# Norm chunks queued behind their roots, tables and tap rows ahead of the second block, down weight pieces ahead of their row pair: one core of a Trainium2 chip

The kernel computes a layer norm, a long convolution branch, a gated MLP branch and all their gradients in one launch. The change moves work in time and adds almost none.

## The chip, the cores and the metric

The program runs on one core of a Trainium2 chip. Times are device microseconds (us) of that core. "Span" is the time of a profiled execution from its first to its last instruction. The engines are called PE (TensorE, matmuls), PEld (its weight loads), DVE (VectorE), ACT (ScalarE), POOL (GpSimd) and SP (SyncE, which issues most DMAs; SPq is its queue of issues).

## The reference

```python
def _B_ref(x, W_gate, W_up, W_down):
    gate = einsum(x, W_gate); up = einsum(x, W_up)
    return einsum(gate * (gate > 0) * up, W_down)      # relu gate
# x = A_q [1, 2048, 1024]; F = 3584; everything is bf16 ... (cut)
xn = _layernorm(x)
out = x + _A_ref(xn, A_k, A_v, A_shift_k, A_ssm_k, A_ssm_D) + _B_ref(xn, W_gate, W_up, W_down)
# _A_ref: k through a 4-tap shift per channel (shift_k), times v, a convolution of
# length 2048 with ssm_k by FFT, plus ssm_D times the same, times xn   ... (cut)
_out, _vjp = jax.vjp(f, A_q, A_k, A_v, A_shift_k, A_ssm_k, A_ssm_D, W_gate, W_up, W_down)
return (_out, *_vjp(grad_out))                          # 10 outputs
```

## The kernel before

`hidden` runs 14 blocks (2 halves of the rows by 7 column blocks of 512). In a block each of 8 row tiles of 128 gets three gemms of 8 matmuls: gate (`ps_g`), up (`ps_u`) and the gradient of the hidden layer (`ps_h`). Their results leave PSUM through four buffers: ACT evicts gate and `ps_h`, DVE evicts up (`ru`). Pieces of the A branch (`steps`) are put between the gemms from some 45 us of matmul work on. Names in the views: `xnT` and `goT` are the normalised rows and the incoming gradient, transposed; `wg`, `wu` and `wdT` the gate, up and down weights; `ru` and `gh` evicted results, which go on to the stores `ug_d` and `h_d`; `hT` is the transposed filter (`ssm_k`), `flp` a transposed intermediate of the FFT, `skb` the tap rows. The first block must also normalise its rows: 10 chunks of one or two row tiles, each loaded by SP, summed by ACT, averaged and scaled by DVE, and transposed by PE (`pst_x`).

```python
LN_CHUNKS = (1, 1, 1, 1, 2, 2, 2, 2, 2, 2)

def layer_norm(...):                       # a generator: three yields a chunk  (cut)
    for i, n in enumerate(self.LN_CHUNKS):
        for j in range(n):
            total = row_sums(j, 0, ACT.Copy)            # ACT  ln_j
        average(0, b(0))                                # DVE  ln_b <- ln_s
        ...                                             # subtract, ACT squares
        yield
        ...
        self.ln_act = nc.scalar.activation(out=f(4), in_=f(3), func=ACT.Sqrt)   # the root
        yield
        ...                                             # reciprocals, scaling on DVE
        yield

def hidden(...):                           # cut to what the change touches
    def up(s, mid=None):
        ...
        self.gemm8(ps, xT[s], wu, mid)
        V.scalar_tensor_tensor(out=ru[s][:, 1, :], in1=ps[:], ...)    # DVE evicts ps_u
    def chunk():
        for _ in range(3):
            next(ln)
    if ahead:                              # the first block
        ...
        yield from first_gate_up(0)
        yield from first_gate_up(2)
        chunk()
    for sp in range(0, HS, 2):             # pairs of row tiles
        if not ahead:
            yield from gate_up(sp)
            load_down(sp // 2)             # a piece of the next block's down weight
        yield from grad(sp)
        if ahead:
            with self.tc.issue_after(self.stored.ins):
                load(6 + sp // 2)          # norm chunks 6 to 9
                if sp == 0:
                    for q in range(4):
                        load_down(q)
        if ahead and sp + 4 < HS:
            yield from gate_up(sp + 4)
            chunk()
        if n == 1 and sp < 4:
            chunk()
            if sp == 2:
                with self.tc.issue_after(self.ln_act.ins), self.tc.issue_after(self.ln_dve.ins):
                    tables()               # DFT tables: ACT sines, DVE index arithmetic

def steps(self):                           # the A branch
    self.pin = True
    nx = self.loads_1(0)
    self.loads_2(nx)
    yield 12000
    self.shift_rows()                      # transpose the taps, copy, store to sk_d
    yield 11000
    self.load_xn(nx)
    self.load_taps(nx)                     # skb <- sk_d
    ...

# main
load(0); load(1); wg; load(2); load(3); wu; load(4); wdT       # in this order, shortened
goT = [b.load_T(g, i, "goT", 8 + i) for i in range(4)]          # transposes by DMA
load(5)
```

`issue_after(x)` lets what is built inside it stand only behind `x` in its queue. After `hidden` come `grad_down`, `grad_in`, `out_phase` and `grad_x`, which the change does not touch.

## Time and profile before

| what | before |
|---|---|
| median of the first 3 runs | 1937.75 us (1937.09 to 1940.97) |
| profiled execution | run 1939.18 us, span 1937.4 us, granted clock 0.996 |
| PE busy | 1893.5 us, with 15294 matmuls and 15526 weight loads recorded |
| DVE, ACT busy | 910.9 and 629.9 us |

PE is the bound, so the useful question is in which stage it is not busy. The view of windows of the kernel before answers that. Its columns are the window and its length, then busy us (and instructions) of PE, PEld, DVE, ACT and POOL, the granted clock of PE, the mean share of busy DMA engines, and GB/s.

```profile
20.00:40.00 20.00, 14.40 (x76) 6.89 (x77) 11.77 (x40) 11.17 (x23) 1.83 (x3) 0.91 1.13 239
40.00:60.00 20.00, 19.89 (x104) 9.57 (x105) 13.03 (x40) 12.82 (x25) 2.14 (x4) 1.00 0.96 271
...
120.00:140.00 20.00, 14.54 (x237) 6.77 (x238) 19.10 (x21) 7.63 (x11) 0.00 (x0) 0.83 0.82 159
```

Two stretches lose over 5 us each (20 to 40 and 120 to 140), and both ran at a lowered clock as well.

### The profile page before, as it was taken

The numbers are of one execution on the slowest core, as the hardware profiler recorded it, in microseconds if no ns is written. First come the engines' busy times: TensorE is split into PE (matmuls) and PEld (weight loads), VectorE is DVE, ScalarE is ACT, GpSimd is POOL, SyncE is SP. The second block draws the span as 40 slices with busy tenths as digits, with TensorE's granted clock in tenths as the row PEclk, the third lists the DMA queues.
The fourth block names the chain that finished last, engine by engine and source line by source line (L and its number), as shares of the span: only waits on it lengthen the run. The fifth ranks groups of instructions, "written<-read, shape, count | busy, mean of one in ns | idle before, by whom it ended". The sixth has DMA issues, their size and how long they took to land.

```text
span 1937.4 us, 35957 instructions
## 1 busy us (share of the span) xinstructions
PE 1893.5 (98%) x15294; PEld 883.2 (46%) x15526; DVE 910.9 (47%) x1378; ACT 629.9 (33%) x863; POOL 15.6 (1%) x38
## 2 busy tenths in 40 slices
PE   8989999999999999999999999999999999999998
PEld 3434444444444444444444444444444444444443
DVE  6677777777677764444444444410122222222222
ACT  5565355355355454344344344311000000000000
POOL 1000000000000000000000000000000000000000
PEclk9999999999999999999999999999999999999999
DMA  9974787974775882654753633384999854554451
GB/s 255 258 168 131 179 186 173 215 196 131 181 188 132 220 249 95 165 141 140 192 153 99 148 119 121 99 241 172 239 259 242 210 130 119 120 122 120 122 118 36
DMA packets 616017, 319.08 MB, mean 165 GB/s; under 512 B 450984, under 2 KB 585136, under 8 KB 615856
## 3 DMA queue, kind: packets, MB, share of 16 engines
q1 hardware_dynamic: 605360, 295.79, 62.2%
q10 hardware_dynamic: 9216, 16.78, 2.8%
q0 software_dynamic: 1280, 4.20, 0.6%
q8 instruction: 121, 1.98, 0.4%
q14 instruction: 40, 0.33, 0.1%
HBM read 141.56 MB, written 95.44 MB: 122 GB/s over the span
## 4 chain that ended last, share of the span: by engine, by line
PE 91%; issue 3%; DMA 2%; SPq 1%; DVE 1%; ACT 1%; ACTq 0%; DVEq 0%; POOLq 0%
PE ps_w L1047 19%; PE ps_x L1229 19%; PE ps_o L1195 10%; PE ps_h L805 9%; PE ps_g L805 9%; PE ps_u L805 9%; PE ps_d L1047 8%; PE ps L72 7%; PE ps_d L1060 1%; SPq L822 1%; PE ps_w L1060 1%; DMA ln_x<-in_A_q_dram 1%; DMA wg<-in_B_W_gate_dram 1%; SPq L816 0%; PE pst L308 0%
## 5 line engine op out<-in xcount | busy, mean ns | idle before, releaser
L1047 PE MATMUL ps_w<-ugs,xn_nat 128*128 128x512 bf16 x1672 | 376.6, 379 | 5.3 <-issue 3.5
L805 PEld LDWEIGHTS <-xnT 128*128 128x128 bf16 x1792 | 171.0, 98 | 211.4 <-issue 12.9
L1047 PEld LDWEIGHTS <-xn_nat 128*128 128x128 bf16 x1728 | 165.0, 98 | 199.3 <-issue 5.5
L805 PE MATMUL ps_g<-wg,xnT 128*128 128x512 bf16 x869 | 204.6, 381 | 5.0 <-issue 1.8
L805 PE MATMUL ps_h<-wdT,goT 128*128 128x512 bf16 x863 | 204.2, 381 | 4.3 <-issue 1.6
L805 PE MATMUL ps_u<-wu,xnT 128*128 128x512 bf16 x866 | 204.5, 380 | 2.4 <-issue 1.3
L1248 ACT ACTIVATE w<-xn,m 128x512 f32<-128x512 bf16 x32 | 24.3, 806 | 559.0 <-issue 317.2
L1229 PE MATMUL ps_x<-wuT,guT 128*128 128x512 bf16 x879 | 197.5, 379 | 0.9
L1229 PE MATMUL ps_x<-wgT,ggT 128*128 128x512 bf16 x878 | 197.3, 379 | 0.9
L1195 PE MATMUL ps_o<-wd,hT 128*128 128x512 bf16 x878 | 192.6, 379 | 0.9
L1047 PE MATMUL ps_d<-g_nat,hs 128*128 128x512 bf16 x741 | 167.7, 379 | 3.1 <-issue 2.5
L1195 PEld LDWEIGHTS <-hT 128*128 128x128 bf16 x896 | 87.7, 98 | 105.7
L1229 PEld LDWEIGHTS <-ggT 128*128 128x128 bf16 x896 | 87.7, 98 | 105.7
L1229 PEld LDWEIGHTS <-guT 128*128 128x128 bf16 x896 | 87.7, 98 | 105.7
L805 PEld LDWEIGHTS <-goT 128*128 128x128 bf16 x896 | 85.7, 98 | 105.1 <-issue 6.3
L319 DVE STREAM_TRANSPOSE flp<-C 128x1024 f32<-128x1024 f32 x48 | 90.5, 1932 | 83.3 <-ACT C L76 83.3
L905 DVE SCALAR_TENSOR_TENSOR ru<-ru,ps_u 128x512 bf16<-128x512 bf16 x112 | 76.7, 684 | 111.1 <-issue 41.7
L966 ACT CAST gh<-ps_h 128x512 bf16<-128x512 f32 x112 | 65.5, 585 | 172.5 <-PE ps_h L805 165.7
L1231 DVE CUSTOM_DVE_ANT_0 gx<-ps_x,gy 128x512 f32<-128x512 f32 x32 | 22.1, 692 | 201.9 <-PE ps_x L1229 192.0
L1145 ACT CAST wi<-ps_w 128x512 bf16<-128x512 f32 x108 | 63.7, 590 | 157.4 <-PE ps_w L1047 149.5
L76 ACT CAST C<-ps 128x1024 bf16<-128x1024 f32 x96 | 92.5, 1015 | 67.2 <-PE ps L72 66.1
L319 DVE STREAM_TRANSPOSE flp<-B 128x1024 f32<-128x1024 f32 x48 | 90.8, 1937 | 47.8 <-ACT B L76 47.8
(170 smaller groups left out, 1518.7 us busy)
## 6 DMA issues: line engine op xcount, KB each, us to landing
ug_d<-ru SPq DMA_DIRECT2D x112, 256.0 KB, 3.0
ugs<-ug_d SPq DMA_DIRECT2D x112, 256.0 KB, 5.6
wg<-in_B_W_gate_dram SPq DMA_DIRECT2D x56, 256.0 KB, 4.3
wu<-in_B_W_up_dram SPq DMA_DIRECT2D x56, 256.0 KB, 4.9
h_d<-ht SPq DMA_DIRECT2D x112, 128.0 KB, 1.8
hs<-h_d SPq DMA_DIRECT2D x56, 256.0 KB, 4.6
out_dram<-wi SPq DMA_DIRECT2D x56, 256.0 KB, 3.0
gt<-in_grad_out_dram SPq DMA_DIRECT2D x32, 256.0 KB, 4.8
```

The source lines that it names most:

```text
L72: self.pri.pin(self.nc.tensor.matmul(out, lhsT=lhsT, rhs=rhs, start=start, stop=stop))
L76: self.pri.pin(self.nc.scalar.copy(out=out, in_=in_))
L319: self.pri.pin(self.nc.vector.transpose(out=df[:, c0:c0 + 32, :], in_=sf[:, c0:c0 + 32, :]))
L805: self.pri.pin(self.nc.tensor.matmul(ps[:], lhsT=xT[:, kt * P:(kt + 1) * P], rhs=w(kt), start=(kt == 0), stop=(kt == self.DT - 1)), always ...
L905: self.pri.pin(nc.vector.scalar_tensor_tensor(out=ru[s][:, 1, :], in0=ru[s][:, 0, :], scalar=0.0, in1=ps[:], op0=ALU.is_gt, op1=ALU.mult))
L966: self.pri.pin(nc.scalar.copy(out=gh[:], in_=ps[:]))
L1047: self.pri.pin(self.nc.tensor.matmul(ps[:], lhsT=lhsT(st), rhs=rhs(st), start=(st == 0), stop=(st == self.ST - 1)))
L1060: self.pri.pin(self.nc.tensor.matmul(ps[i][:], lhsT=lhsT(i, st), rhs=rhs(i, st), start=(st == 0), stop=(st == self.ST - 1)))
L1145: self.pri.pin(nc.scalar.copy(out=wo[0][:, d, :], in_=ps[:]))
L1195: nc.tensor.matmul(ps[:], lhsT=hT[:, kt, :], rhs=self.wd[:, kt, oc], start=(kt == 0), stop=(kt == self.FT - 1))
L1229: nc.tensor.matmul(ps[:], lhsT=T[:, kt, :], rhs=W[:, kt, oc], start=(i == 0), stop=(i == n - 1))
L1248: nc.scalar.activation(out=w[:, oc], in_=xn[:, oc], func=ACT.Identity, scale=m[:, 5:6], bias=m[:, 4:5])
```

## The change

The intent is to close PE's waits in the first 370 us. It has four parts: (1) each norm chunk is queued behind the root of the last one, and the load of chunk 5 goes ahead of two of the gradient's transposes; (2) the tables are built in the first block; (3) the tap rows are transposed and stored at the start of the A branch; (4) pieces of the down weight are loaded ahead of their row pair.

```diff
@@ shift_rows (3)
-        self.act(sk_t[:], ps[:])
-        self.store(self.sk_d, sk_t[:])
+        self.nc.scalar.copy(out=sk_t[:], in_=ps[:])
+        return sk_t
@@ steps (3)
+        sk_t = self.shift_rows()
         self.pin = True
         nx = self.loads_1(0)
         self.loads_2(nx)
-        yield 12000
-        self.shift_rows()
-        yield 11000
+        yield 10000
+        self.load(self.sk_d, sk_t[:])
+        yield 13000
@@ hidden (1)
             def chunk():
-                for _ in range(3):
-                    next(ln)
+                with self.tc.issue_after(self.ln_act.ins):
+                    for _ in range(3):
+                        next(ln)
@@ hidden, the calls of the first block cut
@@ hidden (4)
                 if not ahead:
+                    load_down(sp // 2)
                     yield from gate_up(sp)
-                    load_down(sp // 2)
@@ hidden (2)
                 if n == 1 and sp < 4:
                     chunk()
-                    if sp == 2:
-                        with ...: tables()
+                if ahead and sp == 4:
+                    with ...: tables()
@@ main (1)
-    goT = [b.load_T(g, i, "goT", 8 + i) for i in range(4)]
+    goT = [b.load_T(g, i, "goT", 8 + i) for i in range(2)]
     load(5)
+    goT += [b.load_T(g, i, "goT", 8 + i) for i in range(2, 4)]
```

More of the change, by code (lines that the diff above doesn't have):

```diff
@@ L984, in chunk @@
             def chunk():
+                with self.tc.issue_after(self.ln_act.ins):
+                    for _ in range(3):
+                        next(ln)
+            if ahead:
+                self.warm(24)
                 for _ in range(3):
                     next(ln)
-            if ahead:
-                self.warm(24)
-                chunk()
                 next(ln)
@@ L1017, in hidden @@
                     chunk()
-                    if sp == 2:
-                        with self.tc.issue_after(self.ln_act.ins), self.tc.issue_after(self.ln_dve.ins):
-                            tables()
+                if ahead and sp == 4:
+                    with self.tc.issue_after(self.ln_act.ins), self.tc.issue_after(self.ln_dve.ins):
+                        tables()
             if last:
```

## The prediction

> **What bounds the kernel now.** I read the page first: busy time by engine, then the 40 slices.
>
> ```profile
> PE 1893.5 (98%) x15294; PEld 883.2 (46%) x15526; DVE 910.9 (47%) x1378; ACT 629.9 (33%) x863; POOL 15.6 (1%) x38
> ...
> PE   8989999999999999999999999999999999999998
> ...
> PEclk9999999999999999999999999999999999999999
> ```
>
> TensorE (PE) is busy 98% of 1937.4 us. A change that removes no matmul can win only the idle time of PE, 1937.4 - 1893.5 = 43.9 us, plus matmuls that ran at a lower clock. The slices put the idle time into the first and third slice (48 us each) and the last. The diff removes no matmul, and the two orders of PE's instructions (31054 rows in both kernels) are the same but for the place of one small transpose (of the taps) and buffer names. So the question is which waits of PE it touches. Hence the third view, who PE waited for:
>
> ```profile
> PE pst_x L834 <- DVE ln_x L786: 5.5, 3, 4.5
> ...
> PE ps L72 <- DVE flp L319: 3.2, 1, 3.2
> ...
> PE ps_g L805 <- DVE ru L905: 1.6, 1, 1.6
> ...
> PE ps_h L805 <- DMA wdT<-in_B_W_down_dram: 1.4, 1, 1.4
> ...
> PE ps L72 <- ACT hT L76: 1.2, 1, 1.2
> ```
>
> The columns are total us, times, longest. The rest of PE's list is gaps of 0.2 us ("issue"), and some 8 us lie in the tail after the last matmul; the change touches neither. These five waits are the whole field, and each is aimed at by one part of the diff. Fourth view, the timeline around the two largest; PE first, at 27 us:
>
> ```profile
> 27.50 1.89 PE L805 MATMUL ps_h<-wdT,goT 128*128 128x512 bf16 x8
> 33.92 1.30 PE L834 MATMUL pst_x<-ident,ln_x 128*128 128x128 bf16 x16 [4.54 <-DVE ln_x L786]
> 35.02 2.34 PE L805 MATMUL ps_h<-wdT,goT 128*128 128x512 bf16 x5
> ```
>
> and all engines in the same stretch, for the cause:
>
> ```profile
> 30.91 1.06 ACT L742 ACTIVATE ln_j<-ln_x 128x1024 bf16<-128x1024 bf16 x1 [3.44 <-DMA ln_x<-in_A_q_dram]
> ...
> 31.96 0.19 ACT L774 ACTIVATE ln_s<-ln_s 128x2 f32<-128x2 f32 x1
> ```
>
> The 0.19 us square root (L774) of norm chunk 4 stands on ScalarE behind the first row sum of chunk 5, whose data was issued at 25.50 and landed at 30.9. The root's input was ready at 27.58 (the cast before it on VectorE ends there). The 16 transposes of PE wait for that chunk. Next, the stretch before 135 us, first the cause on VectorE, then PE:
>
> ```profile
> 115.94 1.23 DVE L80 TENSOR_TENSOR ksh<-kp,skb 128x2048 bf16<-128x2048 bf16 x1 [6.92 <-DMA skb<-sk_d]
> ```
>
> ```profile
> 122.50 1.89 PE L805 MATMUL ps_g<-wg,xnT 128*128 128x512 bf16 x8 [1.59 <-DVE ru L905]
> 127.61 1.06 PE L72 MATMUL ps<-flp,FW 64*32 64x128 bf16 x64 [3.23 <-DVE flp L319]
> 129.00 3.19 PE L805 MATMUL ps_g<-wg,xnT 128*128 128x512 bf16 x7 [0.33 <-issue]
> ```
>
> VectorE stood 6.92 us for the tap rows (skb): stored at 109.51, loaded at 113.03. From there it is solidly busy (9.93 of 10 us in 120 to 130), and PE waits for it twice.
>
> **What the Trainium skill says.** (1) "TensorE: Matmul & The Clock Gate", Part 1 (the HAM clock gate): after about one 3.4 us window of idleness the array runs at half clock, 426.7 ns from matmul to matmul at 512 columns instead of 215.7. The trace agrees: 8 in 1.73 us normally (216 ns), but 5 in 2.13 us (426 ns) by the chain of waits after the 4.54 us gap. So a long wait costs more than its length. After the pair 1.59 + 3.23 us it slowed as well, though each is under 3.4; after the lone 1.42 us wait at 366 us it did not. (2) "Perfetto Trace Analysis", Per-engine timelines: VectorE and ScalarE execute strictly in order. The root that is stuck behind a row sum is that. (3) "ScalarE: Activation LUTs", What ACT_TABLE_LOAD costs: about 1283 ns per switch of set, plus a drain. The trace has 1.28 us for the load at 95.44, with the sine 0.02 us after it, so no drain is seen.
>
> **The change part by part.** A full-clock gemm of 8 matmuls is 1.73 us; I measure each loss against that.
>
> *Norm chunk behind the root, sixth load ahead of two gradient transposes.* From ps_h at 27.50 to the first gate matmul at 38.23 is 10.73 us; the work is 2 x 1.73 + 0.89 (16 transposes) = 4.35. Loss 6.38: 4.54 of waiting and some 1.8 of half clock. After: root at about 27.7; then on VectorE in the new order reciprocal (0.16), a small one (0.15), ru (0.69), a small one, ht (0.42), two small ones, with gaps about 2.2 us in all, so the scaling starts near 30.0 and PE's transposes (0.5 after it) near 30.5. PE is ready at 29.2. A wait of about 1.2 us stays, too short for the gate. **Saved: 5.2.**
>
> *Tables earlier.* Before, they ran at 93 to 109 us between the last norm chunk and the first filter work. At 102.02 the copy of hT on ScalarE, whose transposes were done at 101.0, came behind a sine of 1.15 us. In the new order no sine stands there. **Saved: about 1.0 of the 1.2.** VectorE loses 16 us of crowding (9.63 and 8.62 of 10 us busy in 90 to 110). The price: norm roots now fall between sines; ScalarE has 5 table loads instead of 2, 3 x 1.28 = 3.8 us. They fall near 60 to 92 us, where ScalarE is busy 3 to 6 of 10 us, and PE has four PSUM buffers of 1.73 us each before a late eviction stops it. I follow the new order there: evictions come 0.6 to 1.5 us late, with over 3 us to spare. **Cost on the path: 0.**
>
> *Tap rows early.* From ps_h at 119.01 to the second group of flp matmuls at 134.60 is 15.59 us. The work is 2 x 1.73 plus 4.24 (the same group and two gemms in the next round, 134.60 to 138.84) = 7.70. Loss 7.9: 1.8 and 3.4 of waiting, 2.7 of half clock. After: skb lands near 102, so gt, ksh and the taps follow PE's evictions; I put the second flp of VectorE about 2 us ahead of PE's need. **Saved: 7.9.**
>
> *Down weight pieces ahead of their pair.* The wait of 1.42 at 366 us: the piece was issued at 362.49, after two 1.3 us transposes of xn, and needed at 364.6. Ahead of the pair it is there about 7 us earlier. **Saved: 1.4.** The other 55 pieces were hidden already.
>
> Sum: 5.2 + 1.0 + 7.9 + 1.4 = 15.5, so 1937.75 - 15.5 = 1922.3. I add 1.2 for small new waits: **1923.5 us**.
>
> **The rivals.** *A DMA takes the place.* In the first 75 us the DMA engines are busy about all the time (mean share 1.0 to 1.2), and PE comes 5 us earlier. Gate weights of block 1 land about 60 and are needed at 63.3; those of block 2 are issued from 100.34 and needed from 108.67, and the last norm chunk, which the token load ahead of them on the queue waits for, may be 1 us later. Against it: most of these transfers wait for PE to free their buffers and so move with it, and the load queue had some 3 us of idle time at 48 to 53. Worth +1 to +5: about 1927. *VectorE stays the bound at 120 us*: if the taps start only 4 us earlier, PE still waits 2 us and may fall to half clock: +3 to +5, 1927. *The gap at 30 us stays long*, if chunk 4's root waits for something else: +5, 1928. *All is gained*: 6.4 + 1.2 + 7.9 + 1.4 = 16.9 gives 1920.9, the floor. *Table switching stalls PE*: needs an eviction over 3 us late; then 1.28 us per switch, +2 to +4.
>
> **Range and chances.** Two per cent is 38.8 us, over twice all that can be won, and the after-story changes nothing past the first 400 us but DMA order. So within 2% is nearly certain: faster 0.01, same 0.985, slower 0.005. The low end is the floor less 2 us of run spread (before: 1937.1 to 1941.0); the high end has two rivals come true: 1918.5 to 1931.
>
> **What the profile after would show.** PE's wait for ln_x falls from 4.5 to about 1.2; waits for flp, skb and wdT are gone; the clock near 35 and 130 us is full; the tables stand near 60 to 85 us; busy PE stays about 1890 while the span falls 14 us. I am wrong if PE has a new wait over 1 us for wg, wu or goT in the first 130 us, if a wait for ru or gh near 65 to 95 appears, or if the busy time of VectorE still touches PE at 120.

## The result, and the profile after

The changed kernel took 1930.61 us (median of 4 runs, 1927.86 to 1934.58), the kernel before 1937.66 us (4 runs, 1937.09 to 1940.97). The ratio is 0.9962, with a 95% interval of 0.9941 to 0.9982. The result is within 2% and inside the predicted range, but 7 us above the predicted point: about half of the predicted 14.2 us came.

The profiled execution has a span of 1928.7 us at a clock of 0.998. The page of the changed kernel begins with the busy times:

```profile
PE 1909.5 (99%) x15526; PEld 881.6 (46%) x15526; DVE 910.5 (47%) x1378; ACT 633.8 (33%) x866; POOL 15.3 (1%) x38
```

PE's busy time seems to have *grown* by 16 us, with no matmul added. The counts explain it: 15526 matmuls for 15526 weight loads here, but only 15294 for 15526 in the trace of before. That trace had lost 232 matmul records. The second trace of the changed kernel (a0_after, below) settles it: with 15294 matmuls recorded too, PE is busy 1891.9 us there, in a span of 1929.1 us. So a lost record reads as idle time of PE (some of it as the 0.2 us "issue" waits, of which the full trace has none), and the 43.9 us of idle time were overstated by some 17.6 us, what the two traces of one kernel differ by. PE's busy totals can be compared only between traces with equal counts. Stages of the first 140 us can, where few records are lost. The windows of the changed kernel:

```profile
20.00:40.00 20.00, 18.45 (x103) 8.73 (x102) 13.77 (x45) 12.03 (x24) 2.68 (x5) 1.00 1.11 236
40.00:60.00 20.00, 16.62 (x82) 7.63 (x80) 11.16 (x34) 12.38 (x24) 1.07 (x2) 0.91 1.07 288
...
120.00:140.00 20.00, 20.00 (x337) 9.49 (x335) 12.86 (x15) 13.43 (x18) 0.00 (x0) 1.00 0.88 167
```

The bad stretches of before are repaired: PE rose from 14.40 to 18.45 us and from 14.54 to 20.00 us of 20, at full clock. But 40 to 60, which was full, now has the hole and the lowered clock (0.91, just what 20 to 40 had before). The list of PE's waits in the changed kernel (total us, times, longest) names it:

```profile
PE ps_h L806 <- DVE ru L906: 3.4, 1, 3.4
PE pst_x L835 <- DVE ln_x L787: 2.4, 4, 0.8
PE ps_u L806 <- DMA wu<-in_B_W_up_dram: 1.7, 1, 1.7
...
PE ps L72 <- ACT hT L76: 0.2, 1, 0.2
```

The long wait for `ln_x`, and the waits for `flp` and `wdT`, are gone; the one for `hT` has shrunk to 0.2. In their place stand one of 3.4 us for `ru` and one of 1.7 us for `wu`. PE's timeline of the changed kernel around the first (start, length, instructions, the wait before them in brackets):

```profile
27.02 1.89 PE L806 MATMUL ps_h<-wdT,goT 128*128 128x512 bf16 x8
29.67 1.07 PE L835 MATMUL pst_x<-ident,ln_x 128*128 128x128 bf16 x16 [0.76 <-DVE ln_x L787]
...
40.98 1.06 PE L835 MATMUL pst_x<-ident,ln_x 128*128 128x128 bf16 x16
45.41 3.56 PE L806 MATMUL ps_h<-wdT,goT 128*128 128x512 bf16 x8 [3.38 <-DVE ru L906]
48.77 3.67 PE L806 MATMUL ps_g<-wg,xnT 128*128 128x512 bf16 x16
```

The norm gap is down to 0.76 us. PE therefore reaches the `pst_x` of the next tile at 40.98; before it was there at 46.86, about 6 us later. Then it waits 3.38 us, and its next gemm runs at half clock (3.56 us in place of 1.89). The same stretch on the other engines tells why:

```profile
28.18 6.91 SPq L823 DMA_TRANSPOSE goT<-in_grad_out_dram  x4
...
36.29 0.41 SPq L723 DMA_DIRECT2D ln_x<-in_A_q_dram  x1
...
41.26 1.06 ACT L743 ACTIVATE ln_j<-ln_x 128x1024 bf16<-128x1024 bf16 x1 [4.66 <-DMA ln_x<-in_A_q_dram]
...
43.48 0.17 DVE L757 TENSOR_SCALAR ln_b<-ln_s 128x2 bf16<-128x2 f32 x1 [4.54 <-ACT ln_j L743]
...
44.69 0.68 DVE L906 SCALAR_TENSOR_TENSOR ru<-ru,ps_u 128x512 bf16<-128x512 bf16 x1
```

Read it from the top. Four gradient transposes hold SP for 6.91 us, stores follow, and SP issues the load of norm chunk 6 at 36.29; it lands at about 41.2. ACT waits 4.66 us for it, and DVE waits for ACT's sums. Behind that average (L757), in DVE's order, stands `ru` (L906), the eviction that must free the PSUM buffer for PE's `ps_h`. So DVE stands idle with an eviction in its queue, and PE waits behind it. In the kernel before the same queue and the same engine show:

```profile
27.61 7.20 SPq L822 DMA_TRANSPOSE goT<-in_grad_out_dram  x4
...
36.07 0.40 SPq L722 DMA_DIRECT2D ln_x<-in_A_q_dram  x1
```

```profile
42.38 1.05 ACT L742 ACTIVATE ln_j<-ln_x 128x1024 bf16<-128x1024 bf16 x1
```

The load was issued at 36.07, behind four gradient transposes that hold SP for 7.20 us and behind stores, and in the changed kernel it comes at the same time (36.29, behind the same transposes). But before, ACT came to it at 42.38 and found it there. The compute moved about 6 us earlier and the load did not.

The stretch of the taps (PE, changed kernel) has no wait left:

```profile
118.13 1.90 PE L806 MATMUL ps_h<-wdT,goT 128*128 128x512 bf16 x8
...
121.69 0.75 PE L72 MATMUL ps<-flp,FW 64*32 64x128 bf16 x64
...
125.93 0.75 PE L72 MATMUL ps<-flp,FW 64*32 64x128 bf16 x64
```

From `ps_h` to the second `flp` group it is 125.93 - 118.13 = 7.80 us, where it was 15.59.

The balance of the two profiles, each gap against its work as the prediction counts it:

| stretch | loss before | loss after | saved | predicted |
|---|---|---|---|---|
| norm chunk at 30 us | 6.38 | 0.97 | 5.4 | 5.2 |
| `hT` at 102 us | 1.19 | 0.23 | 1.0 | 1.0 |
| taps at 120 us | 7.89 | 0.10 | 7.8 | 7.9 |
| `wdT` at 366 us | 1.42 | 0 | 1.4 | 1.4 |
| start (first loads, differs from run to run) | | | 0.5 | |
| chunk 6 at 42 us: wait 3.4, half clock 1.6, rest 0.2 | 0 | 5.2 | -5.2 | |
| weights: `wu` 1.7 at 257 us, `wg` 0.8 at 108 us | 0 | 2.5 | -2.5 | |
| sum | | | 8.4 | 15.5, less 1.2 |

The spans differ by 1937.4 - 1928.7 = 8.7 us, so the balance closes within 0.3 us. (5.2 is 7.79 us from 40.98 to 48.77 less 16 transposes, 0.89, and one gemm, 1.73. The 0.8 for `wg` is read from the time between the third and the fourth pair of `hT` matmuls, with one gate gemm between them: 106.60 to 109.52 is 2.92 us, and before it was 108.23 to 110.39, 2.16 us. The list of waits shows only 0.2 of it.)

### The profile page after: what moved, and what is told of

It is laid out like the page before. It is cut to its first block, busy times and chain, and to the rows that moved or that the text cites. A ratio compares the mean times of both kernels' runs of the same rounds, so it can differ in the third digit from the quotient of the medians.

```text
span 1928.7 us, 36213 instructions
## 1 busy us (share of the span) xinstructions
PE 1909.5 (99%) x15526; PEld 881.6 (46%) x15526; DVE 910.5 (47%) x1378; ACT 633.8 (33%) x866; POOL 15.3 (1%) x38
## 4 chain that ended last, share of the span: by engine, by line
PE 96%; issue 1%; DMA 1%; DVE 1%; ACT 1%; DVEq 0%; SPq 0%; ACTq 0%
PE ps_w L1050 20%; PE ps_x L1232 19%; PE ps_o L1198 10%; PE ps_h L806 10%; PE ps_u L806 10%; PE ps_g L806 10%; PE ps_d L1050 9%; PE ps L72 7%; PE ps_d L1063 1%; PE ps_w L1063 1%; ACT ln_j L743 0%; PE pst L308 0%; DMA ln_x<-in_A_q_dram 0%; DMA wu<-in_B_W_up_dram 0%; DMA wg<-in_B_W_gate_dram 0%
## 5 line engine op out<-in xcount | busy, mean ns | idle before, releaser
L1050 PE MATMUL ps_w<-ugs,xn_nat 128*128 128x512 bf16 x1728 | 383.7, 379 | 0.0
L1050 PE MATMUL ps_d<-g_nat,hs 128*128 128x512 bf16 x768 | 171.9, 379 | 0.0
L319 DVE STREAM_TRANSPOSE flp<-C 128x1024 f32<-128x1024 f32 x48 | 90.5, 1931 | 83.3 <-ACT C L76 83.3
L906 DVE SCALAR_TENSOR_TENSOR ru<-ru,ps_u 128x512 bf16<-128x512 bf16 x112 | 76.5, 683 | 110.3 <-issue 48.6
L319 DVE STREAM_TRANSPOSE flp<-B 128x1024 f32<-128x1024 f32 x48 | 90.9, 1939 | 47.8 <-ACT B L76 47.8
```

Source lines behind the costliest of these rows:

```text
L319: self.pri.pin(self.nc.vector.transpose(out=df[:, c0:c0 + 32, :], in_=sf[:, c0:c0 + 32, :]))
L906: self.pri.pin(nc.vector.scalar_tensor_tensor(out=ru[s][:, 1, :], in0=ru[s][:, 0, :], scalar=0.0, in1=ps[:], op0=ALU.is_gt, op1=ALU.mult))
L1050: self.pri.pin(self.nc.tensor.matmul(ps[:], lhsT=lhsT(st), rhs=rhs(st), start=(st == 0), stop=(st == self.ST - 1)))
```

## The experiments

**The theories.** Theory 1: the norm part only moves PE's wait from chunk 5 to chunk 6's load, so it is worth nothing unless the loads move too. Its rival: the norm part brings its 5 us, and something else loses them. A second dispute is over each part's share, above all whether the early tables earn their place. The first four runs shared one chip (before: 1937.13 us, 11 runs); the others shared another (before: 1939.86 and 1939.73 us). I compare ratios, with 95% intervals. All kernels gave correct results.

| label | kernel | median us | ratio to before |
|---|---|---|---|
| a0_after | changed kernel again | 1930.3 | 0.9962 [0.9948, 0.9976] |
| e1_load6 | changed, load of chunk 6 early | 1930.64 | 0.9961 [0.9945, 0.9977] |
| e2_loads_all | changed, loads 6 to 9 each a step early | 1929.51 | 0.9955 [0.9941, 0.9970] |
| e3_norm_only | before + part 1 | 1939.48 | 1.0007 [0.9993, 1.0021] |
| e4_taps_only | before + part 3 | 1931.95 | 0.9963 [0.9951, 0.9975] |
| e6_no_down | changed less part 4 | 1933.26 | 0.9969 [0.9956, 0.9982] |
| e9_loads_tabback | e2 less part 2 | 1926.0 | 0.9931 [0.9919, 0.9944] |
| e10_loads_sines | e2, last norm chunks behind the sines | 1928.24 | 0.9943 [0.9930, 0.9955] |
| e7_down_only | before + part 4 | 1936.0 | 0.9982 [0.9966, 0.9998] |
| e8_tables_back | changed less part 2 | 1930.83 | 0.9952 [0.9936, 0.9969] |
| e12_norm_loads | before + part 1 + early loads | 1935.03 | 0.9978 [0.9963, 0.9992] |
| e13_best | e9, A branch started 3.5 us later | 1929.6 | 0.9949 [0.9936, 0.9963] |

Part 2 alone was not run; e8 and e9 stand for it.

### a0_after: the changed kernel again

No edit.

> The changed kernel again, to have its time on the chip of the runs beside it and a second profile. Median near 1930.6 us (so far 1927.9 to 1934.6). If the 3.4 us wait near 42 us and the half clock after it are systematic, both are there again within 0.5 us; the 1.7 us wait for wu near 256 us may come and go if it is a matter of DMA traffic.

Measured: 0.9962, as at first. The new wait is there again (3.13 us), and the half clock after it lasts longer: over the eight `ps_h` and into the next gate matmuls (16 in 4.77 us in place of 3.62). For `wg` PE loses time again (107.63 to 111.65 is 4.02 us where 2.16 is the work, 1.9 us lost), and it does not wait at all for `wu` at 257 us. So the hole at 42 us belongs to the kernel, and so does a late `wg`, in differing size (see e9); the wait for `wu` comes and goes between runs of one kernel.

### e3_norm_only: part 1 without the others

```diff
 # kernel before, with the hunks (1) of the change: chunk() behind ln_act, load(5) between the goT pairs
```

> Kernel before with only the norm part (each chunk behind the last root, sixth load ahead of two gradient transposes). Theory 1 (the wait was moved, not removed): the gap near 29 us shrinks by 5.4 us, a new one of 5.2 us opens near 42 us, net 0 to -0.5, near 1937.3 us. Rival (this part keeps its own gain and the loss near 42 us comes of the tables or taps): 1937.7 - 5.4 = 1932.3 us.

Measured: 1.0007, no gain. PE's wait at 29 us fell to 0.75 us, as in the changed kernel, and PE's timeline of this run shows what took its place:

```profile
46.30 2.52 PE L805 MATMUL ps_h<-wdT,goT 128*128 128x512 bf16 x7 [4.06 <-DVE ru L905]
```

The wait that was removed came back at 46 us, and the gemm behind it took 2.32 us (to 48.62) in place of 1.73. Theory 1 holds: by itself, part 1 moves a wait and earns nothing.

### e1_load6: the suspected load early

```diff
     load(5)
+    load(6)
     goT += [...]
@@
-                        load(6 + sp // 2)
+                        if sp:
+                            load(6 + sp // 2)
```

> Changed kernel with the token load of norm chunk 6 issued right behind that of chunk 5 (near 22 us instead of 36.3). Theory 1 (the gap near 42 us is that load, late because four gradient transposes hold the queue from 28.2 to 35.1 us): the wait of 3.4 us and the half clock are gone, -5.2 us, 1925.4 us. Theory 1b (the next chunk's load, left where it is, then takes its place near 52 us): -1 to -3 us, 1928 to 1929. Rival (the order of VectorE or the queueing behind the root makes the gap whatever the load does): no change, 1930.6.

Measured: 0.9961. The cause is confirmed and the gain is missed. The hole at 42 us is gone, but the time did not follow. PE's timeline of this run, and in the second fence the other engines' around its wait at 57.94:

```profile
42.10 1.89 PE L806 MATMUL ps_h<-wdT,goT 128*128 128x512 bf16 x7
...
57.94 1.89 PE L806 MATMUL ps_h<-wdT,goT 128*128 128x512 bf16 x8 [1.86 <-DMA wg<-in_B_W_gate_dram]
...
92.43 1.89 PE L806 MATMUL ps_h<-wdT,goT 128*128 128x512 bf16 x8 [0.92 <-ACT ru L900]
```

```profile
53.78 1.06 ACT L743 ACTIVATE ln_j<-ln_x 128x1024 bf16<-128x1024 bf16 x1 [1.47 <-DMA ln_x<-in_A_q_dram]
...
56.01 0.17 DVE L757 TENSOR_SCALAR ln_b<-ln_s 128x2 bf16<-128x2 f32 x1 [5.59 <-ACT ln_j L743]
...
57.21 0.68 DVE L906 SCALAR_TENSOR_TENSOR ru<-ru,ps_u 128x512 bf16<-128x512 bf16 x1
```

`ps_h` follows its transposes at once (42.10), and the next long row of `ps_h` begins at 50.74, where it began at 55.73 and 56.75 in the two traces of the changed kernel. PE is 5 to 6 us ahead. Then it gives that back in pieces: chunk 7's load is now the late one, in the same pattern: ACT waits for it until 53.78, DVE's average waits for ACT, `ru` stands behind, and PE starts 0.05 us after `ru` ends at 57.89. (The profile puts the 1.86 us down to `wg`, which this gemm does not read: the releaser that it names is the last that it saw.) Four waits of 0.4 to 0.9 us for evictions follow between 71 and 93 us. When PE comes to the filter's transposes it is at 99.34 us, against 99.16 and 100.18 in the changed kernel. Closing the hole exposed the next load and then ACT and DVE.

### e2_loads_all: all the later chunk loads a step early

```diff
     load(5)
+    load(6)
     goT += [...]
@@
-                        load(6 + sp // 2)
+                        load(7 + sp // 2)
```

> Changed kernel with the token loads of chunks 6 to 9 each issued one step earlier. Theory 1: at least as good as the run that moves only chunk 6, 1925.4 us; if the next chunk's load is the next bound (theory 1b) this run is 2 to 4 us faster than the one that moves only chunk 6. Rival (order, not the load): 1930.6. If the added early traffic hurts gate weights or transposes: slower than 1927.

Measured: 0.9955, not distinguishable from the changed kernel, so the expected gain was missed again. PE still waits for evictions on ACT (0.79 us at 53, then 0.4 and 0.9 us up to 92 us). In 80 to 90 us ACT is busy 9.40 of 10 us (its row is shown under e9): the tables' sines, two of the three additional switches of table (the third comes at 91.66) and the norm sums all stand there. But ACT is as busy there in the changed kernel (9.41), where PE does not wait; the busy share alone proves nothing. ACT's timeline says more, first of e2, then of the changed kernel. The lines with `ln_s` are roots, of chunk 7 (near 59) and of chunk 9 (near 93):

```profile
52.56 0.60 ACT L900 ACTIVATE ru<-ps_g 128x512 bf16<-128x512 f32 x1 [6.42 <-DMA ug_d<-ru]
...
59.08 0.21 ACT L775 ACTIVATE ln_s<-ln_s 128x2 f32<-128x2 f32 x1 [0.18 <-DVE ln_s L774]
...
92.95 0.20 ACT L775 ACTIVATE ln_s<-ln_s 128x2 f32<-128x2 f32 x1
```

```profile
59.26 0.20 ACT L775 ACTIVATE ln_s<-ln_s 128x2 f32<-128x2 f32 x1 [0.18 <-DVE ln_s L774]
...
93.11 0.20 ACT L775 ACTIVATE ln_s<-ln_s 128x2 f32<-128x2 f32 x1
```

Chunk 7's root comes at the same time in both, although PE is 5 us ahead in e2: the eviction before that chunk's sums waited 6.42 us for a store of `ug_d`. (The store issued at 48.81 fits, behind four transposes of `wdT` that held SP from 39.57 to 48.71. No run moved it.) And from that root to chunk 9's it is 33.9 us in both, as in a0_after, e1 and e6, however early PE comes. New theory (2): with the loads moved, this chain on ACT and DVE under the early tables is the next bound. Its rival: ACT is busy by coincidence and the DMA binds.

### e9_loads_tabback: e2 with the tables in their old place

```diff
+                    if sp == 2:
+                        with ...: tables()
-                if ahead and sp == 4:
-                    with ...: tables()
```

> Changed kernel with the loads of chunks 6 to 9 a step earlier and the tables back behind the last norm chunk. Theory 2 (with the loads early, ScalarE is the bound from 60 to 94 us, by sines and table loads between the norm chunks): PE reaches the transposes of hn near 94 to 95 us instead of 98.6, its waits for ru and gh near 53 to 92 us are gone or below 0.5 us in sum; the tables then stand in front of the filter and part is given back: 1925 to 1928 us. Rival (DMA is the bound of that stretch: gate weights, token loads): transposes still at 98 to 99 us, 1929 to 1931.

Measured: 1926.0 us, 0.9931. This is the fastest kernel and beats both kernels: its interval lies wholly below that of the changed kernel's second run. The windows of e2 and then of e9 (columns as above):

```profile
80.00:90.00 10.00, 9.54 (x45) 4.24 (x44) 6.73 (x21) 9.40 (x17) 1.09 (x2) 1.00 1.19 229
```

```profile
80.00:90.00 10.00, 9.95 (x47) 4.53 (x47) 6.19 (x25) 6.62 (x13) 0.72 (x2) 1.00 1.08 205
```

ACT falls from 9.40 to 6.62 of 10 us and PE rises from 9.54 to 9.95. At the filter's transposes PE is at 95.46 us, against 98.59 in e2. Chunk 9's root follows chunk 7's by 28.1 us (58.78 to 86.86) in place of 33.9. The cost is that PE's wait for `hT` behind the sines is back. PE's waits of e9:

```profile
PE ps L72 <- ACT hT L76: 1.4, 1, 1.4
...
PE ps_h L806 <- DVE ru L906: 0.4, 1, 0.4
```

Theory 2 holds for the larger part: step by step, PE of e2 loses 2.2 us against e9 between 74 and 92 us, where evictions are late under the sines. The rival has a part too: 0.6 us at 53 us, behind the store, and 0.6 at 60 to 65 us, for weights. (The eviction waits left in e9 sum to 0.6 us; below 0.5 was expected.)

A second cost of the early tables is only partly in the lists of waits (0.2 of 0.8 us in the changed kernel, nothing in e6). It lies at the gate weights of the next block, between the third and the fourth pair of `hT` matmuls. PE's timeline of e2 and then of e9:

```profile
106.03 0.60 PE L72 MATMUL ps<-hT,RH 128*128 128x512 bf16 x2
...
110.96 0.59 PE L72 MATMUL ps<-hT,RH 128*128 128x512 bf16 x2
```

```profile
104.03 0.59 PE L72 MATMUL ps<-hT,RH 128*128 128x512 bf16 x2
...
106.20 0.59 PE L72 MATMUL ps<-hT,RH 128*128 128x512 bf16 x2
```

That is 4.93 us against 2.17. The stretch takes 2.15 to 2.17 us in all seven traces with late tables and this order of gemms (before, e3, e4, e7, e8, e9, e12), and 2.85 to 4.93 us in all six with early tables (changed kernel 2.92 and 4.02, e6 2.85, e1 3.52, e10 3.55, e2 4.93). On SP the loads of `wg` stand behind a token load (`xt`) that reads what the last norm chunk has stored. With early tables that chunk's root is late (93.11 in the changed kernel, 91.21 before), the token load goes out at 98.42 in place of 97.27, and the first `wg` is issued 3.4 us after PE's filter transposes in place of 0.5. (The load of the tap rows, part 3, stands in front of it too; it does so in e4 and e9 as well, without loss.)

So once the loads are early, the early tables cost 3.1 us by 99 us and 2.8 more at `wg`, and save 1.1 at `hT`: 4.8 us in all, of the 5.4 us between the two spans (1929.2 and 1923.8).

### e10_loads_sines: fewer table switches instead

```diff
 # e2, with tables() returning its last sine (trB)
-                        tables()
+                        self.ln_act = tables()     # the next norm chunks stand behind the last sine
```

> Changed kernel with the loads of chunks 6 to 9 a step earlier and all sines ahead of the two last norm chunks, so that ScalarE loads tables 3 times instead of 5 (2.56 us less). Theory 2: PE's transposes of hn near 96 us instead of 98.6, waits for ru and gh below half of 2.5 us, 1926.5 to 1928 us. Rival (ScalarE's table loads cost nothing on the path, DMA bounds): 1929.5 us as without it.

Measured: 0.9943. The table loads fell from 5 to 3, but PE reached the filter's transposes at 98.71 us, as in e2, not at the expected 96. PE's timeline shows the small waits gathered into one:

```profile
79.72 3.61 PE L807 MATMUL ps_h<-wdT,goT 128*128 128x512 bf16 x16 [1.95 <-ACT ru L901]
```

Some 1 us of this was lost before the tables, where chunk 5's load landed late in this trace and PE waited 0.95 us at 33 us. But from 65 to 93.5 us, where the tables stand, e10 takes no less than e2 either: 64.68 to 93.53 against 65.27 to 93.41, the same gemms. Fewer switches, bought with norm sums that stand behind the sines, thus win nothing there, while moving the whole tables does (e9). Which part of their work binds is not separated; ACT also waits 2.92 us for DVE's index arithmetic. Whether e10 is a little faster than e2 is open, as their intervals overlap.

### e8_tables_back: the changed kernel without part 2

```diff
 # changed kernel, with the hunk (2) undone, as in e9
```

> Changed kernel with only the tables put back behind the last norm chunk (loads of chunks 6 to 9 late, as in the change). Theory: with the loads late PE comes late enough that the sines cost it nothing, so moving the tables is worth its 1.0 us for hT and no more: ratio to before 0.9967, 1.0 us above the changed kernel; the gap near 42 us is there. Rival (the moved tables cost PE time in the change too): as fast or faster than the changed kernel, ratio 0.996 or below.

Measured: 0.9952, against 0.9962 with the part; the intervals overlap. The hole at 42 us is 4.1 us here and `hT`'s wait 1.2 us. Moving the tables earned nothing measurable. The traces show why: it saves 1.0 us at `hT` and loses 0.8 us (1.9 in a0_after) at `wg`, where e8 loses nothing (2.15 us between the pairs of `hT` matmuls). Which of the two is larger in the mean, the times do not show.

### e4_taps_only: part 3 alone

```diff
 # kernel before, with the hunks (3) of the change: shift_rows and steps
```

> Kernel before with only the tap rows stored and loaded early; tables, norm and down pieces as before. Theory (the taps are nearly the whole gain of the change): both waits of PE near 122 to 128 us and the half clock after them are gone, -7.9 us, near 1929.3 us, as fast as the whole change. Rival (the tables, still at 93 to 109 us, keep VectorE late): half of it, 1933.

Measured: 0.9963, the whole gain of the change, with the tables still in their old place: the rival (half of the gain) is out. PE has no wait for `flp` or `ru` left at 120 us; its waits show that the other three places stay as they were (for `ln_x` 5.8 us at the longest, `hT` 1.2), for instance:

```profile
PE ps_h L806 <- DMA wdT<-in_B_W_down_dram: 2.0, 1, 2.0
```

### e7_down_only and e6_no_down: part 4 alone, and the change without it

```diff
 # e7: kernel before, with the hunk (4)        e6: changed kernel, with the hunk (4) undone
```

> Kernel before with only the down weight pieces ahead of their row pair. Theory: the 1.4 us wait near 366 us goes and nothing else: ratio to before 0.9993. Rival (the moved pieces delay gate or up weights in other blocks): new waits for wg or wu, ratio 1.000 or more.

> Changed kernel with the down weight pieces back behind their pair. Theory: the 1.4 us wait for wdT near 360 us is back and nothing else changes, 1930.3 + 1.4 = 1931.7 us. Rival (the moved pieces cause the new waits for gate and up weights near 108 and 256 us, 0.2 to 2 us): those are gone and the time is equal or lower, 1929 to 1930.5.

Measured: 0.9982 alone, and 0.9969 without it against 0.9962 with it. In e7 the wait for `wdT` is gone and no new wait for weights appears; in e6 it is back at 1.6 us. The traces confirm its 1.4 us. The times agree with that but cannot prove it: 0.0007 of 1939 us is 1.4 us, with overlapping intervals, and e7's 0.9982 reaches from 0.4 to 6.6 us. The rival of e6, that the moved pieces cause the late `wg`, is out: that stretch takes 2.85 us in e6, near the 2.92 of the changed kernel.

### e12_norm_loads: part 1 with the loads it needs

```diff
 # e3, with the edits of e2 on the loads
```

> Kernel before with the norm part of the change and the loads of chunks 6 to 9 a step earlier, nothing else. Theory 1 (the norm part is worth its 5.4 us and more once the load behind it is not the next bound): 5 to 6.5 us faster than before, ratio 0.9970; the same part without the loads gave 1.0007. Rival (a third bound takes it back): ratio above 0.999.

Measured: 0.9978, where part 1 without the loads had 1.0007. The difference is 0.0029, some 5.6 us. There is no hole at 42 us and PE reaches the filter's transposes at 94.57 us (before: 99.82). Against the kernel before, the ratio says 4.3 us (1.6 to 7.2), less than the 0.9970 that was expected. So part 1 can bring about what the prediction gave it (5.2), but only with the loads. The taps' waits stay, since part 3 is missing. One of them is instructive for the clock; the view is PE's timeline:

```profile
117.67 3.47 PE L805 MATMUL ps_g<-wg,xnT 128*128 128x512 bf16 x8 [2.01 <-DVE ru L905]
```

Eight matmuls took 3.47 us in place of 1.89, after a lone wait of only 2.01 us.

### e13_best: can e9's last waits be closed by a later A branch?

```diff
-A_START = 45_000
+A_START = 48_500
```

> The fastest version so far (loads early, tables back, ratio 0.9931) with the whole convolution branch started 3.5 us later, so that the copy of hT comes behind the sines instead of between them. Theory: the 1.4 us wait for hT goes, ratio 0.9925. Rival (the copy now stands behind the two last sines too and the wait grows, or the shift of the branch makes others): ratio 0.993 or above.

Measured: 0.9949, slower than e9. The copy of `hT` met the next sines, its wait grew from 1.4 to 3.75 us, and the clock was halved after it. The theory was wrong and its rival right; e9 remains the best.

## Why the prediction was right, and where it was off

- **"A change that removes no matmul can win only the idle time of PE"** held, and so did the forecast of within 2%. The figure of 43.9 us for that idle time was overstated, because 232 matmul records were missing. "Busy PE stays about 1890" looks wrong for the same reason (1909.5), and holds between traces with equal counts (1893.5 and 1891.9). I had the two counts side by side in the first line that I quoted and did not use them. The "31054 rows" stand in no trace (a full one has twice 15526), and "the rest of PE's list is gaps of 0.2 us" passed over waits of 1.5, 0.8 and 0.8 us, which both kernels have.
- **Norm chunk, "Saved: 5.2"**: 5.4 in its own stretch, with a wait of 0.8 where 1.2 was expected. Locally right, and e12 shows that the time is there to be had.
- **Tables, "Saved: about 1.0", "Cost on the path: 0"**: the 1.0 is in the trace. The zero cost held at 60 to 92 us only because PE stood at 42 us and came late; no eviction wait appeared there in the changed kernel. In e1 and e2, where PE came earlier, such waits of 0.4 to 0.9 us appeared, and moving the tables back won 3.1 us by 99 us. And the late last norm chunk did cost 0.8 us at `wg`. The claim of "over 3 us to spare" was true of a stretch that another wait had slowed.
- **Tap rows, "Saved: 7.9"**: 7.8, at full clock. e4 shows that this part alone gives the time of the whole change.
- **Down weight pieces, "Saved: 1.4"**: 1.4 in the trace.
- **"I add 1.2 for small new waits"** is the step that failed. It measured 7.7: 5.2 at chunk 6's load and 2.5 at weights. The rival "A DMA takes the place" was the right one, though larger than its +1 to +5. What it said of the gate weights of block 2 and the token load came true in small (0.8); but it did not name the norm load, and I argued it away with "the load queue had some 3 us of idle time at 48 to 53". That queue was not idle from 25 to 47 us, where the load in question was issued. "Most of these transfers wait for PE to free their buffers and so move with it" did not hold for that load: it waited behind transposes and stores on its own queue and was issued at 36.1 us before and at 36.3 us in the changed kernel.

None of the signs of being wrong fired: there was no wait over 1 us for weights or `goT` in the first 130 us, none for `ru` or `gh` at 65 to 95, and none for DVE at 120. The hole was a wait for `ru` at 42 us, which no sign watched, and the span fell by 8.7 us in place of 14. That the range held is partly luck. Its high end, 1931, had two rivals come true; the one that did come true was larger than its size, the median of 1930.61 lies 0.4 us inside, and single runs reach 1934.58.

**What stays open.** The wait for `wu` near 257 us was 1.7 us in one profile of the changed kernel and 0.5 in e2, and is in no other list of waits; no run settles its cause. Why the loss at `wg` differs so much among kernels with early tables (0.7 to 2.8 us) is open too. The parts alone add up to +0.0007 - 0.0037 - 0.0018 = -0.0048, which is what the change without the tables shows (0.9952) and a little more than the change itself (0.9962). That would fit a small cost of the early tables there, as at `wg`, but the intervals do not separate it.

## What to carry to other kernels

When a wait is taken away, redo the same reading one stage later with the new arrival time: take the next loads in the order of their queue, compare each one's landing with when its data will now be asked for, and look at what stands behind that consumer in an in-order engine. Slack that was measured while another wait slowed the kernel (here ACT in 60 to 92 us) is not slack once that wait is gone. Compare stretches of equal work between two traces, and not only their lists of waits: much of the loss at `wg` was in no list. Run each part alone and with what it needs: here one part brought all of the gain, and another was worth nothing until four loads were issued one step earlier (together with late tables: 1926.0 us).

## What the Trainium skill lacked or had wrong

- "TensorE: Matmul & The Clock Gate", Part 1, gives about one 3.4 us window of idleness before the clock falls. Here a lone wait of 2.01 us was enough (e12: 8 matmuls in 3.47 us, at a granted clock of 0.50 from 118 to 121 us), while waits of 2.10 us (e3), 1.70 us (changed kernel) and 1.42 us (before) did not slow PE. The page does call the window free-running; a rule that fits these runs is that a wait of about 2 us may or may not halve the clock.
- "ScalarE: Activation LUTs", What ACT_TABLE_LOAD costs, adds a drain to the 1283 ns, for 2.66 us a switch. In e1 the load starts at 82.49 and the root behind it at 83.78, and the next load follows the root's end within 0.03 us: 1.28 us a switch, with no drain to be seen.
- "Perfetto Trace Analysis" does not warn that lost matmul records show as idle time of PE: the two traces of the changed kernel have 15294 and 15526 matmuls for 15526 weight loads, and PE busy for 1891.9 and 1909.5 us. Comparing the two counts first would show it.
